# A new order of attention's steps, and the passage of an MLP to its seven products

## The chip, the cores and the metric

One core of one Trainium2 chip runs the whole program as one launch. The metric is device time in microseconds (us); lower is better. The times of the kernel before are from 3 runs: 1110.34, 1112.88 and 1113.99, so the median is 1112.88.

## What is computed

Three layers follow each other on a tensor of 4 batches, 576 positions and 512 channels (before the first layer there are 1152 positions).

```python
# 1: attention of 4 x 8 heads with 64 channels; q is averaged over pairs of positions
q_pool = q.reshape(B, H, S // 2, 2, D).mean(axis=3)          # S = 1152 -> T = 576
scores = scale * np.matmul(q_pool, k.transpose(0, 1, 3, 2))  # 576 x 1152 a head
attn   = softmax(scores);  x = attn @ v
# 2: four expert attentions (64 channels, causal), mixed by the two best gates of a position
# 3: a mixing over positions of rank 32, u = x + U, V part, and
ch  = np.maximum(u @ w_ch1, 0.0) @ w_ch2                     # 512 -> 2048 -> 512
out = u + ch
```

The two MLP matrices arrive as 64-bit floats.

## The kernel before, in words

**Precision.** Where a plain product is not accurate enough, the kernel splits an operand into a rounded high part and a low part (`cut`: ACT writes the high part, the named engine subtracts to get the low one) and multiplies three of the four combinations.

**Attention** goes over 16 pairs of heads. A pair has 2 halves of the queries (288 each) and 9 blocks of 128 keys, thus 18 units (`unit`), each with two scores (one for each head of the pair): 36 steps. `score` issues two matmuls of 128 x 288 (L606, L607) into a buffer `st` of PSUM, then ACT's exponential (L608) into `pt`, and after the second head POOL's addition to the sum `acc` (L615, L618). `pv` (L626) multiplies `pt` with the values; it is not issued unit by unit but in batches, because a group of units waits until the step that the table PV_AT gives for each unit.

Beside the 36 steps of a pair the next pair is prepared (`prep`): loads of q, k and v (`load_q`, `load_k` L482, `load_v`, one buffer for k), the sum of q's position pairs, transposes on PE (L506 for k, L515 for q), a layout of q and k by transfers from SBUF to SBUF (lines L547 to L549, L377 and L378, twelve a pair), a bound for the maximum of each row of scores (36 tests: a matmul L558 against `bd` and a DVE maximum L560) and the negated bound `nm` (L410, L412, sent on by L415). The transfers into `bd` are L537. All DMAs are issued from SP's queue in the order written, and one that waits holds up those behind it. The constants at the head of the file (LQ_AT, K_AT, SECOND_AT, ...) say at which step each piece is issued; a negative step lies in the pair before. PE, DVE and ACT take their instructions in the order written. WC_AT and WD_AT place the decoding of the first 64-bit weights (loads, and integer steps on DVE, L244 to L248) in the same steps; POST_AT places the division after a half (`post_a` L633, `post_r` L432 to L435, `post_b` L445 and L643).

**The expert attention** takes over after about 470 us with the same kind of stream; its first products read `xh` and `xl`, a cut of attention's output (`xl` on DVE at L227).

**The MLP** handles the 2304 positions in 6 groups x of 384. Groups 0 and 1 run in a base loop of T1 = 28 ticks: a tick has one up product (`up` L1199, 12 matmuls), one down product (`down` L1218, 9 matmuls, one tick after its up), and the work that the list `todo` names for the tick (`more`): decoding of a weight block, and preparations for the second part. There the groups 2 to 5 run as two passes p of 8 steps k of `seven`: seven products instead of eight on combined blocks of weights (`combine`) and of activations. The activations are transposed on PE (L1155), copied by ACT to SBUF (`lift`, L1173), and added and cut in a second step (`blend`: sums L1191 and cuts L227, shared between DVE and POOL). `seven` issues the products m5, m3, m1, m2, m4, m6, m7 (L1268) and adds them up on DVE (L1280) into four blocks that go through the ReLU and the second matrix. The products use a pool `ms` of three PSUM buffers, of which one is held as part of the output of an odd group. In this part POOL and SP also take their instructions in the order written.

Of the kernel before, what the change touches and what calls it, by code (L numbers as in the profile page):

```python
# [20 lines left out]
LQ_AT = -41  # L21
LK_AT = -19
V_AT = 5
Q_AT = [-5, -1]
K_AT = [-2, 3, 10]
LAY_AT = 18
FIRST_AT = [-33, -20, -20, -15, -10, -10, -7, -7, -6, -5, -3, 10, 13]
SECOND_AT = [-12, -9, -6, -2, 4, 11, 14, 6, 7, 9, 12, 12, 14, 15, 16, 16, 17, 17, 17, 19, 21, 21, 21, 24, 24, 25, 28, 28, 30, 31, 34, 36, 36, 36, 29, 42]
M_AT = [2, 5, 6, 7, 8, 9, 11, 12, 12, 13, 15, 16, 17, 18, 19, 20, 21, 25, 26, 28, 29, 29, 32, 32, 35, 36, 37]
F_AT = [23, 40]  # L30
PV_AT = [11, 11, 11, 16, 16, 16, 16, 31, 31, 31, 31, 31, 31, 31, 35, 35, 35, 35]
POST_AT = [[31, 32, 35], [47, 48, 53]]

WL_AT = 10
WC_AT = [10, 17, 32, 35]
WD_AT = [18, 33, 37, 39]
# [87 lines left out]
def kernel(  # L124
# [898 lines left out]
    def open_late():  # L1023
        xes.close()
        ct["cw1"] = pool(ctx, "cw1", LW)
        ct["bc"] = pool(ctx, "cbc", 8)
        ct["u"] = pool(ctx, "cu", 2)
        ct["e"] = pool(ctx, "ce", 8)
        ct["t"] = pool(ctx, "ctm", 2)
# [47 lines left out]
    def split(fi):  # L1077
        for x, g in enumerate([weights(fi, x) for x in range(2)]):
# [8 lines left out]
            "m6": (2, 0, ALU.subtract), "m7": (1, 3, ALU.subtract)}  # L1087
# [70 lines left out]
    def turn(x, c):  # L1158
# [3 lines left out]
    MOVE, STG, tn = {}, {}, [0]  # L1162
    QUAD = ((0, 0), (0, 1), (1, 0), (1, 1))
    MOVES = {"m1": (0, 3, ALU.add), "m2": (0,), "m3": (2, 3, ALU.subtract), "m4": (1, 0, ALU.subtract), "m5": (3,),
             "m6": (0, 2, ALU.add), "m7": (1, 3, ALU.add)}

    def lift(p, ci, d):

        x, h = QUAD[d]
        if d == 0:  # L1170
            STG[p, ci] = ct["bc"].tile([P, 4, TB], F32, name="sg", tag="bc") if p == 1 and ci else \
                xpool.tile([P, 4, TB], F32, name="sg", tag="x")
# [255 lines left out]
```

## Time and profile before

| what | value |
|---|---|
| median of 3 runs | 1112.88 us |
| the profiled execution | 1115.27 us |
| its span from first to last instruction | 1113.5 us |
| PE busy | 1078.2 us (97%) |
| DVE, POOL, ACT busy | 811.9, 613.1, 542.8 us |
| granted clock of PE, mean | 0.989 |

PE is the engine that is nearly always busy, so time is to be found where it waits and where the clock granted to it is below 1.00. All starts below count from the span's start. Attention's pairs follow each other about every 27.7 us, pair 0 from 18.5 us on; the MLP's base loop covers some 735 to 850 us.

### The profile page before, as it was taken

To read this page: it belongs to the slowest core of one execution; us is meant where nothing else is said; L and a number is where in the kernel's file an instruction comes from. 1 tells how busy PE (TensorE), PEld (TensorE's weight loads), DVE (VectorE), ACT (ScalarE), POOL (GpSimd) and SP (SyncE) were. 2 spreads that over 40 slices of the span, in tenths; PEclk is the share of its full clock that TensorE was granted. 3 is DMA by queue.
4 is the path that set the end of the run, shared out by engine and by line. 5 is a ranking of instruction groups with operands and counts; after the bars stand their busy time and mean duration, and the time that the engine had idled before them with its cause. 6 is when DMAs were issued, how large, how long until landed. Compare 5 with 4: busy or idle time off the path is not lost.

```text
span 1113.5 us, 19597 instructions
## 1 busy us (share of the span) xinstructions
PE 1078.2 (97%) x6652; PEld 889.9 (80%) x6652; DVE 811.9 (73%) x1707; ACT 542.8 (49%) x1361; POOL 613.1 (55%) x620
## 2 busy tenths in 40 slices
PE   6999999999999999899999998899998999999998
PEld 4777777777777777688888886699887888999987
DVE  6777777888888777566868779969879555564444
ACT  4555556555555555544555454534445445432231
POOL 5778989988887888864524244200009596800000
PEclk8999999999999999999999999999999999999999
DMA  6867888878777675012222243466665745575431
GB/s 145 193 160 179 187 197 194 182 170 187 179 172 169 159 162 129 23 35 54 63 71 59 71 134 136 139 208 199 218 203 184 241 167 196 192 265 195 165 123 58
DMA packets 135157, 171.50 MB, mean 154 GB/s; under 512 B 72464, under 2 KB 88848, under 8 KB 133008
## 3 DMA queue, kind: packets, MB, share of 16 engines
q1 hardware_dynamic: 135056, 170.24, 56.2%
q8 instruction: 53, 0.87, 0.4%
q14 instruction: 48, 0.39, 0.1%
HBM read 83.06 MB, written 32.51 MB: 104 GB/s over the span
## 4 chain that ended last, share of the span: by engine, by line
PE 82%; DVE 7%; POOL 5%; DMA 3%; issue 2%; ACT 2%; SPq 0%; POOLq 0%; ACTq 0%; DVEq 0%
PE o L1218 13%; PE pv L626 12%; PE ms L745 9%; PE ms L1268 8%; PE st L606 8%; PE ms L558 7%; PE st L607 6%; PE ms L1199 5%; PE pv L896 2%; PE ms L633 2%; PE st L871 1%; DVE mp L560 1%; POOL cb L227 1%; PE ms L506 1%; PE st L872 1%
## 5 line engine op out<-in xcount | busy, mean ns | idle before, releaser
L618 POOL TENSOR_TENSOR acc<-acc,pt 128x576 f32<-128x576 f32 x224 | 319.3, 1426 | 34.9 <-ACT pt L608 20.4
L608 ACT ACTIVATE pt<-st 128x288 f32<-128x288 f32 x576 | 219.8, 409 | 188.3 <-PE st L607 143.6
L560 DVE TENSOR_REDUCE mp<-ms 128x1 f32<-128x384 f32 x432 | 215.1, 549 | 59.8 <-PE ms L558 57.8
L626 PE MATMUL pv<-pt,vr 128*64 128x288 f32 x1152 | 154.0, 413 | 0.0
L558 PE MATMUL ms<-kn,bd 128*128 128x384 f32 x432 | 146.1, 362 | 3.9 <-DVE mp L560 1.7
L626 PEld LDWEIGHTS pv<-pt,vr 128*64 128x64 f32 x1152 | 80.7, 138 | 56.3 <-issue 5.2
L1218 PE MATMUL o<-w,hh 128*128 128x512 f32 x384 | 121.4, 396 | 1.0 <-POOL w L227 0.7
L606 PE MATMUL st<-q1a,s1a 128*128 128x288 f32 x288 | 93.7, 325 | 1.4 <-ACT pt L608 1.1
L606 PE MATMUL st<-q1b,s1b 128*128 128x288 f32 x288 | 92.7, 322 | 0.2 <-ACT pt L608 0.2
L558 PEld LDWEIGHTS ms<-kn,bd 128*128 128x128 f32 x432 | 80.7, 194 | 14.7 <-DVE mp L560 5.5
L607 PE MATMUL st<-q2a,s2a 128*128 128x288 f32 x288 | 85.4, 296 | 0.0
L607 PE MATMUL st<-q2b,s2b 128*128 128x288 f32 x288 | 85.3, 296 | 0.0
L1268 PE MATMUL ms<-bc,w 128*128 128x384 f32 x432 | 84.8, 341 | 0.0
L1218 PEld LDWEIGHTS o<-w,hh 128*128 128x128 f32 x384 | 72.1, 190 | 13.8 <-POOL w L227 1.5
L1268 PEld LDWEIGHTS ms<-bc,w 128*128 128x128 f32 x432 | 77.6, 190 | 3.0
L1218 PE MATMUL o<-w,hl 128*128 128x512 f32 x192 | 75.9, 395 | 1.2 <-DVE hl L1203 1.2
L1199 PE MATMUL ms<-uh,w 128*128 128x384 f32 x256 | 74.1, 350 | 2.8 <-POOL w L227 1.1
L606 PEld LDWEIGHTS st<-q1a,s1a 128*128 128x128 f32 x288 | 54.6, 190 | 24.2 <-issue 21.1
L888 POOL TENSOR_TENSOR acc<-acc,pt 128x576 f32<-128x576 f32 (+4 forms) x48 | 44.3, 923 | 51.0 <-ACT pt L879 49.4
L1218 PE MATMUL o<-w,hs 128*128 128x512 f32 x288 | 71.4, 393 | 0.0
L615 POOL TENSOR_TENSOR acc<-pt 128x576 f32<-128x576 f32 x32 | 50.7, 1585 | 37.3 <-ACT pt L608 37.3
L227 POOL TENSOR_TENSOR bc<-sg,bc 128x384 fp32r<-128x384 f32 x6 | 7.0, 1173 | 109.7 <-ACT bc L226 109.7
(241 smaller groups left out, 2408.3 us busy)
## 6 DMA issues: line engine op xcount, KB each, us to landing
raw<-in_moe_w_ch_dram SPq DMA_DIRECT2D x32, 512.0 KB
w_d<-cb SPq DMA_DIRECT2D x40, 256.0 KB
qr<-in_q_dram SPq DMA_DIRECT2D x16, 576.0 KB
vr<-in_v_dram SPq DMA_DIRECT2D x16, 576.0 KB
s1a<-kn SPq DMA_DIRECT2D x31, 288.0 KB
s1b<-kn SPq DMA_DIRECT2D x31, 288.0 KB
kr<-in_k_dram SPq DMA_DIRECT2D x30, 288.0 KB
wv<-v_d SPq DMA_DIRECT2D x8, 1024.0 KB
```

Source lines behind the costliest of these rows:

```text
L558: nc.tensor.matmul(ps[:, :384], BD[i % 2][:, t, :], KN[i % 2][:, c * 384:c * 384 + 384], start=True, stop=True)
L560: nc.vector.tensor_reduce(st["mp"][:, t, c:c + 1], ps[:, :384], axis=X, op=ALU.max)
L606: nc.tensor.matmul(ps[:, :HT], pr.S1[a][:, ks], pr.Q1[a][:, qs], start=True, stop=False)
L607: nc.tensor.matmul(ps[:, :HT], pr.S2[a][:, ks], pr.Q2[a][:, qs], start=False, stop=True)
L608: nc.scalar.activation(c["pt"][:, a, :], ps[:, :HT], AF.Exp, scale=0.0625)
L615: nc.gpsimd.tensor_add(t, acc[i, h], c["pt"])
L618: nc.gpsimd.tensor_add(acc[i, h], acc[i, h], c["pt"])
L626: nc.tensor.matmul(o[64 * a:64 * a + 64, :HT], vr[:, a, kt, :], c["pt"][:, a, :], start=(kt == 0), stop=(kt == NKT - 1))
L745: nc.tensor.matmul(ps, stat[x][s], mov[x][m], start=(x == 0 and y == 0), stop=(x == n - 1 and y == 2))
L1199: nc.tensor.matmul(ps[:, :TB], W[fi][:, 0, a, cs], m[:, c, :], start=(c == 0 and y == 0), stop=(c == NC - 1 and y == 2))
L1218: nc.tensor.matmul(ob[x][s_], hl[m][:, r], w2[a], start=(n == 0 and y == 0), stop=(n == NF - 1 and y == 2))
L1268: nc.tensor.matmul(ps[:, :TB], w[:, i * HD2 + c * P:i * HD2 + c * P + P], b[:, j, c, :], start=(c == 0 and y == 0), stop=(c == HC - 1 and ...
```

## The change

**Tables.** Every table of attention's order has new numbers. The batches of PV have 4, 4, 7 and 3 units (3, 4, 7 and 4 before), at steps 11, 15, 32 and 35 (11, 16, 31, 35). The layout moves from step 18 to 22, k's load from -19 to -30, and the second part of a division from 53 to 50 in the second half. Two lines of the diff stand for the rest.

```diff
-LK_AT = -19
+LK_AT = -30
-PV_AT = [11, 11, 11, 16, 16, 16, 16, 31, 31, 31, 31, 31, 31, 31, 35, 35, 35, 35]
-POST_AT = [[31, 32, 35], [47, 48, 53]]
+PV_AT = [11, 11, 11, 11, 15, 15, 15, 15, 32, 32, 32, 32, 32, 32, 32, 35, 35, 35]
+POST_AT = [[32, 33, 35], [47, 48, 50]]
...
-WC_AT = [10, 17, 32, 35]
-WD_AT = [18, 33, 37, 39]
+WC_AT = [10, 14, 30, 32]
+WD_AT = [23, 31, 34, 35]
```

**Lifts.** Two of the four blocks (d = 0 and 3) are copied to SBUF by ACT; the other two are never copied, but DVE adds them from PSUM to the copied ones. There is one lift a tick, from T1 - 9 on, and its cuts come one tick later; for the second pass there is one every second tick, with the cuts' low part on POOL. `blend` is gone.

```diff
-    def lift(p, ci, d):
+    def lift(p, ci, d, eng):
...
-        nc.scalar.activation(STG[p, ci][:, d], turn_(2 * p + x, h * HC + ci), AF.Copy)
-
-    def blend(p, ci, m, eng):
...
+        ps = turn_(2 * p + x, h * HC + ci)
+        if d in (0, 3):
+            nc.scalar.activation(sg[:, d // 3], ps, AF.Copy)
+        todo_ = {0: (), 3: (("m1", 0, ALU.add),), 1: (("m4", 0, ALU.subtract), ("m7", 1, ALU.add)),
+                 2: (("m3", 1, ALU.subtract), ("m6", 0, ALU.add))}[d]
+        ts = {}
+        for m, y, op in todo_:
+            ts[m] = ct["t"].tile([P, TB], F32, name="tb")
+            nc.vector.tensor_tensor(ts[m], ps, sg[:, y], op=op)
+
+        def rest():
+            if d in (0, 3):
+                t = move(p, ("m2", "m5")[d // 3])
+                cut(sg[:, d // 3], t[:, 0, ci], t[:, 1, ci], eng)
+            for m in ts:
+                t = move(p, m)
+                cut(ts[m], t[:, 0, ci], t[:, 1, ci], eng)
...
-    for y in range(8):
-        at(T1 - 11 + y // 2, lambda y=y: lift(1, y // 4, y % 4))
-        at(T1 + 4 + y + 10 * (y // 4), lambda y=y: lift(2, y // 4, y % 4))
-    for y in range(14):
-        m, ci = PIECES[y // 2], y % 2
-        at(T1 - 7 + y if y < 3 else T1 - 4 + (y - 3) // 3,
-           lambda y=y, m=m, ci=ci: blend(1, ci, m, nc.gpsimd if y % 3 == 1 else nc.vector))
-        at(T1 + 8 + y + 7 * (y // 7), lambda y=y, m=PIECES[y % 7]: blend(2, y // 7, m, nc.gpsimd))
+    for y, (ci, d) in enumerate((ci, d) for ci in range(HC) for d in (0, 3, 1, 2)):
+        at(T1 - 9 + y, lambda ci=ci, d=d: lift(1, ci, d, nc.vector))
+        at(T1 + 7 + 2 * y, lambda ci=ci, d=d: lift(2, ci, d, nc.gpsimd))
```

**Combined weights and temporaries.** `combine` takes its engine; for k = 0 that is DVE instead of POOL. The temporaries of `seven` get a pool of their own (`m`, 5 buffers; the pool `e` goes from 8 to 3), and some sums are made in place. The cut of the block c12 is issued before m1 instead of behind it.

```diff
-            nc.gpsimd.tensor_tensor(t, v_[:, x], v_[:, y], op=op)
+            eng.tensor_tensor(t, v_[:, x], v_[:, y], op=op)
...
-            at(s1 - 5 + y * 4 // 7, lambda k=k, m=m: combine(k, m))
+            at(s1 - 5 + y * 4 // 7, lambda k=k, m=m: combine(k, m, nc.gpsimd if k else nc.vector))
```

**Second products kept back.** The last two down products of the base loop (groups 0 and 1, block 15) are not issued at its end but handed to the first `seven`, which issues one behind m5 and one behind m1. The closing additions of groups 0 and 1 follow there.

```diff
-    def mlp(x, fi):
+    def mlp(x, fi, full=True):
         hl = up(x, fi)
-        if pend:
+        if pend and full:
             down(*pend.pop())
...
-            mlp(x, fi)
-            close()
+            mlp(x, fi, t + 1 < T1)
             more()
-        down(*pend.pop())
-        late = []
+        late = list(pend)
```

Three places of the resulting order follow. The first is SP's queue in pair 0, from the first layout of a prepared pair on (`q1a_161` to `s2b_160` are its tiles, `kr` the next keys). Before:

```order
L415 DMA q2a_149<-nm 1x4x64
L415 DMA q2b_150<-nm 1x4x64
L547 DMA q1b_162<-qh 64x576
L548 DMA q1b_162<-ql 64x576
L549 DMA q2b_164<-qh 64x576
L377 DMA s1a_157<-kn_142 64x1152 x2
L378 DMA s2a_159<-klo 64x1152
L377 DMA s1b_158<-kn_142 64x1152 x2
L378 DMA s2b_160<-klo 64x1152
L482 DMA kr<-in_k_dram 128x9x64 x2
L415 DMA q2a_163<-nm 1x5x64
L415 DMA q2b_164<-nm 1x5x64
```

And in the changed kernel, from the same load of the values on:

```order
L489 DMA vr<-in_v_dram 128x2x576
L482 DMA kr<-in_k_dram 128x9x64 x2
L415 DMA q2a_149<-nm 1x4x64
L415 DMA q2b_150<-nm 1x4x64
L547 DMA q1a_161<-qh 64x576
L548 DMA q1a_161<-ql 64x576
L549 DMA q2a_163<-qh 64x576
L547 DMA q1b_162<-qh 64x576
L548 DMA q1b_162<-ql 64x576
L549 DMA q2b_164<-qh 64x576
L377 DMA s1a_157<-kn_142 64x1152 x2
L378 DMA s2a_159<-klo 64x1152
```

The two loads of `kr` stood behind the twelve transfers of the layout and now stand ahead of them and of `nm`.

The second place is SP's queue shortly behind it, where the raw q of a later pair (`qr`) and the blocks of `bd` are moved. Before:

```order
L415 DMA q2a_163<-nm 1x5x64
L415 DMA q2b_164<-nm 1x5x64
L473 DMA qr<-in_q_dram 96x2x768
L537 DMA bd_137<-qh 64x6x64 x2
L537 DMA bd_137<-qh 64x3x64 x2
L489 DMA vr<-in_v_dram 128x2x576
```

In the changed kernel:

```order
L537 DMA bd_137<-qh 64x6x64 x2
L415 DMA q2a_163<-nm 1x5x64
L415 DMA q2b_164<-nm 1x5x64
L473 DMA qr<-in_q_dram 96x2x768
L537 DMA bd_137<-qh 64x3x64 x2
L489 DMA vr<-in_v_dram 128x2x576
```

The first transfers of `bd` were behind `qr` and are now ahead of `nm` and of `qr`.

The third place is PE where the base loop ends (`o_0_9622` to `o_2_9624` are the outputs of one group, `o_0_9942` or `o_0_9945` and so on of the other). Before, from the last down product but one on:

```order
L1218 MATMUL o_1_9623<-w,hl 128x512
L1218 MATMUL o_2_9624<-w,hh 128x512 x2
L1218 MATMUL o_2_9624<-w,hl 128x512
L1218 MATMUL o_0_9942<-w,hh 128x512 x2
L1218 MATMUL o_0_9942<-w,hl 128x512
L1218 MATMUL o_1_9943<-w,hh 128x512 x2
L1218 MATMUL o_1_9943<-w,hl 128x512
L1218 MATMUL o_2_9944<-w,hh 128x512 x2
L1218 MATMUL o_2_9944<-w,hl 128x512
L1268 MATMUL ms<-bc,cb 128x384 x6
L1268 MATMUL ms<-bc,w 128x384 x6
L1268 MATMUL ms<-bc,cb 128x384 x12
```

In the changed kernel, from the last matmul of the last up product on:

```order
L1198 MATMUL ms<-uh_9498,w 128x384
L1267 MATMUL ms<-bc,cb 128x384 x6
L1217 MATMUL o_0_9622<-w,hh 128x512 x2
L1217 MATMUL o_0_9622<-w,hl 128x512
L1217 MATMUL o_1_9623<-w,hh 128x512 x2
L1217 MATMUL o_1_9623<-w,hl 128x512
L1217 MATMUL o_2_9624<-w,hh 128x512 x2
L1217 MATMUL o_2_9624<-w,hl 128x512
L1267 MATMUL ms<-bc,w 128x384 x6
L1267 MATMUL ms<-bc,cb 128x384 x6
L1217 MATMUL o_0_9945<-w,hh 128x512 x2
L1217 MATMUL o_0_9945<-w,hl 128x512
```

The first product of `seven` (6 matmuls) now follows the last up product at once, one of the two kept-back down products stands between it and the second, and the other behind the third.

## Rows read from the trace of the kernel before

**Rows 1.** the page: busy time of each engine; one group of its fifth part
```profile
PE 1078.2 (97%) x6652; PEld 889.9 (80%) x6652; DVE 811.9 (73%) x1707; ACT 542.8 (49%) x1361; POOL 613.1 (55%) x620
...
L560 DVE TENSOR_REDUCE mp<-ms 128x1 f32<-128x384 f32 x432 | 215.1, 549 | 59.8 <-PE ms L558 57.8
```

**Rows 2.** stretches: us, busy us of each engine, PE's granted clock, DMA share, GB/s
```profile
47.60:79.00 31.40, 29.53 (x197) 22.28 (x195) 21.44 (x45) 16.01 (x45) 21.58 (x16) 0.95 0.74 163
247.44:275.16 27.72, 27.72 (x199) 21.49 (x196) 22.76 (x46) 16.25 (x47) 23.83 (x19) 1.00 0.80 187
330.50:359.70 29.20, 28.26 (x200) 21.60 (x196) 25.77 (x49) 15.82 (x45) 23.41 (x18) 1.00 0.72 168
```

**Rows 3.** timeline of PE, pair 0: start, us, engine, line, tiles [idle before]
```profile
53.94 0.52 PE L506 MATMUL ms<-ident,kr 128*128 128x128 f32 x3 [1.78 <-DVE xt L643]
...
54.82 3.85 PE L626 MATMUL pv<-pt,vr 128*64 128x288 f32 x16
...
69.44 2.16 PE L626 MATMUL pv<-pt,vr 128*64 128x288 f32 x16
```

**Rows 4.** timeline of SP's transfer issues, pair 0
```profile
44.91 2.91 SPq L482 DMA_DIRECT2D kr<-in_k_dram  x2
```

**Rows 5.** waits of PE in pair 3: engine, line, releaser, us, times, longest
```profile
PE ms L558 <- DMA bd<-qh: 1.2, 1, 1.2
```

**Rows 6.** timeline of DVE and PE, pair 10 and an earlier pair
```profile
235.73 0.17 DVE L434 TENSOR_SCALAR d<-d 128x9 f32<-128x9 f32 x1
...
346.70 1.45 DVE L434 TENSOR_SCALAR d<-d 128x9 f32<-128x9 f32 x1
...
348.86 0.45 PE L558 MATMUL ms<-kn,bd 128*128 128x384 f32 x1 [0.74 <-DVE mp L560]
```

**Rows 7.** timeline of DVE and PE, passage to the second attention
```profile
458.06 7.19 DVE L227 TENSOR_TENSOR xl<-xt,xh 128x576 fp32r<-128x576 f32 x4 [2.24 <-ACT xh L226]
465.18 0.47 DVE L445 STREAM_TRANSPOSE d<-d 128x288 f32<-128x288 f32 x1
465.68 0.75 DVE L643 TENSOR_TENSOR xt<-pv,d 128x288 f32<-128x288 f32 x1
...
463.43 0.41 PE L745 MATMUL ms<-xl,wqk 128*128 128x320 f32 x1 [0.66 <-DVE xl L227]
...
465.31 0.42 PE L745 MATMUL ms<-xl,wqk 128*128 128x320 f32 x1 [1.18 <-DVE xl L227]
```

**Rows 8.** timeline of PE and DVE, passage to the seven products
```profile
848.26 0.50 PE L1218 MATMUL o<-w,hl 128*128 128x512 f32 x1 [0.93 <-DVE hl L1203]
...
856.54 1.84 PE L1268 MATMUL ms<-bc,cb 128*128 128x384 f32 x6 [3.24 <-DVE c L1280]
...
855.93 0.56 DVE L1280 TENSOR_TENSOR c<-ms,m5s 128x384 f32<-128x384 f32 x1 [0.75 <-ACT m3s L1277]
```

**Rows 9.** chain that ended last, same passage: start, us, what
```profile
853.63 1.14 POOL tw L1123
...
856.54 3.76 PE ms L1268 x12
```

**Rows 10.** the same chain in ticks of the base loop
```profile
785.63 2.08 PE o L1218 x9
787.71 2.12 PE ms L1199 x12
...
805.62 0.34 PE ms L1155 x3
```

**Rows 11.** a tick without lifts, and one with two
```profile
783.52:787.71 4.19, 4.19 (x23) 3.80 (x22) 3.78 (x8) 1.89 (x5) 0.00 (x0) 1.00 0.91 254
...
803.52:808.89 5.37, 5.12 (x29) 4.43 (x28) 3.70 (x7) 2.45 (x5) 0.00 (x0) 1.00 0.15 59
```

**Rows 12.** DVE by line and form, 829 to 856: busy us, mean ns
```profile
L1191 DVE TENSOR_TENSOR tb<-sg 128x384 f32<-128x384 f32 x4 | 4.5, 1160 | 0.0
```

**Rows 13.** timeline of DVE, tick 26
```profile
835.39 0.55 DVE L227 TENSOR_TENSOR bc<-u,bc 128x384 fp32r<-128x384 f32 x1
```

More of the change, by code (lines that the diff above doesn't have):

```diff
@@ L1027, in open_late @@
         ct["u"] = pool(ctx, "cu", 2)
[L1028 to L1029 removed]
+        ct["e"] = pool(ctx, "ce", 3)
+        ct["m"] = pool(ctx, "cm", 5)
+        ct["t"] = pool(ctx, "csg", 2)
     W, V1 = {}, {}
@@ L1160, in turn, with move @@
         cut(turn_(x, c), UH[x][:, c, :], UL[x][:, c, :])
-    MOVE, STG, tn = {}, {}, [0]
+    MOVE, STG = {}, {}
     QUAD = ((0, 0), (0, 1), (1, 0), (1, 1))
-    MOVES = {"m1": (0, 3, ALU.add), "m2": (0,), "m3": (2, 3, ALU.subtract), "m4": (1, 0, ALU.subtract), "m5": (3,),
-             "m6": (0, 2, ALU.add), "m7": (1, 3, ALU.add)}
-    def lift(p, ci, d):
[L1169 to L1172, printed above, removed]
-        nc.scalar.activation(STG[p, ci][:, d], turn_(2 * p + x, h * HC + ci), AF.Copy)
-    def blend(p, ci, m, eng):
-        if ci == 0:
+    def move(p, m):
+        if (p, m) not in MOVE:
             n = PIECES.index(m)
@@ L1180, in blend @@
             MOVE[p, m] = q.tile([P, 2, HC, TB], F32R, name="bc", **kw)
-        d, sg = MOVE[p, m], STG[p, ci]
-        if len(MOVES[m]) == 1:
-            t = sg[:, MOVES[m][0]]
-        else:
-            tn[0] += 1
-            if p == 1 and tn[0] % 2:
-                t = SPARE[0][:, tn[0] // 2 % 2]
-            else:
-                t = ct["t"].tile([P, TB], F32, name="tb")
-            x, y, op = MOVES[m]
-            eng.tensor_tensor(t, sg[:, x], sg[:, y], op=op)
-        return lambda: cut(t, d[:, 0, ci], d[:, 1, ci], eng)
+        return MOVE[p, m]
+    def lift(p, ci, d, eng):
+        x, h = QUAD[d]
+        if d == 0:
+            STG[p, ci] = ct["t"].tile([P, 2, TB], F32, name="sg", bufs=1)
+        sg = STG[p, ci]
+        ps = turn_(2 * p + x, h * HC + ci)
[14 more added lines that the diff above has]
+                cut(ts[m], t[:, 0, ci], t[:, 1, ci], eng)
+        return rest
     def up(x, fi):
@@ L1287, in seven @@
         mul("m3")
-        copy("m3")
-        add("c12", "m3", "m5s")
+        copy("m3", "c22")
+        add("c12", "m3", "c11")
+        h12 = spread_h(s["c12"])
         mul("m1")
-        add("c22", "m1", "m3s")
-        add("c11", "m1", "m5s", ALU.subtract)
-        h12 = spread_h(s["c12"])
+        add("c11", "m1", "c11", ALU.subtract)
+        add("c22", "m1", "c22")
         if late:
@@ L1298, in seven @@
         mul("m2")
-        copy("m2")
-        add("c22", "c22", "m2", ALU.subtract)
+        copy("m2", "c21")
+        nc.vector.tensor_tensor(s["c22"], s["c22"], s["m2"][:, :TB], op=ALU.subtract)
         mul("m4")
-        add("c21", "m4", "m2s")
-        add("c11", "c11", "m4")
+        add("c21", "m4", "c21")
+        add("c11", "m4", "c11")
         h21 = spread_h(s["c21"])
```

78 lines of the change are left out of this document (35 added, 43 removed).

## The prediction

> **What bounds the kernel now.** I read the page first: PE is busy 1078.2 of 1113.5 us [rows 1], so all its idle time is 35.3 us. DVE is next with 811.9. A change that leaves PE's matmuls as they are (this one does: the same products in another order) can win only from that idle time and from stretches in which PE ran at its lower clock; it can lose only where PE comes to wait. So I went through PE's waits and matmul times stage by stage. The reader is to see three things. A steady pair of heads lasts 27.72 us with PE busy all of it [rows 2]. Pairs 0 and 10 of the same work last longer, and each contains a wait of PE [rows 2]. And the longest wait outside the start, 3.24 us, stands where the MLP goes over to the seven products [rows 8].
>
> **Steady pairs.** PV batches of 3, 4, 7, 4 units become 4, 4, 7, 3: four batches before and after, so PE changes from scores to PV as often. With PE busy all 27.72 us there is no idle time to remove; price 0. It would cost something only if a moved step made PE wait (rival 1).
>
> **Pair 0.** PE stops 1.78 us before the transposes of kr [rows 3]. The row names DVE's xt, but that product was long done; by the order these transposes wait for the two loads of kr. SP issued those only at 44.91 [rows 4], because they stand behind the twelve transfers that lay out q and k, and behind two of nm between them. After the stop the 16-matmul PV batch took 3.85 us [rows 3]; a batch of the same form took 2.16 at 69.44 [rows 3], and the granted clock, 1.00 (2.4 GHz) all through a steady pair, is 0.95 as a mean of this stretch, so that part of it ran at 1.2 GHz [rows 2]. So the stop costs 1.78 + 1.69 = 3.5 us, and the 31.40 us of this stretch less 27.72 (3.7) agrees. In the changed order the loads of kr stand ahead of nm and of the twelve transfers: −3.5. What becomes late next are those transfers, now behind nm and behind kr's 2.91 us of issuing; see rival 3.
>
> **Pair 3.** PE waits 1.2 us for bd [rows 5]. In the new queue the first loads of bd stand ahead of qr: −1.2.
>
> **Pair 10.** It takes 29.20 against 27.72 [rows 2], 1.5 us more. Half is one wait for DVE's maxima, 0.74 [rows 6]; there DVE spent 1.45 us on a scaling of 9 columns, which took 0.17 at 235.73 [rows 6]. The decoding steps (WC) move away from this place, ahead of the batches, but still in every pair; I take 60%: −0.9, with ends 0 and −1.5.
>
> **To the second attention.** DVE's four subtractions xl take 7.19 us in a row, and PE waits 0.66 and 1.18 us on the last two [rows 7]. The second part of the division (transpose 0.47 and product 0.75, [rows 7]) moves from behind the fourth xl to between the second and the third. PE then gets the third and fourth 1.22 us later: +1.2.
>
> **Start.** The first steps move from ahead of the first pair into it (11 negative places, now 7). Four tests of 549 ns [rows 1] are 2.2 us that DVE no longer has to do before the first scores, and has to do during them; nothing in the trace of before shows which wins. Price 0, ends −2.2 and +2.2.
>
> Attention: −3.5 − 1.2 − 0.9 + 1.2 = −4.4.
>
> **The turn to the seven products.** PE waits 0.93 for hl and 3.24 for c [rows 8], and the 12 matmuls after the second wait take 3.76 us [rows 9] against 2.12 for 12 matmuls of the same 384 columns earlier [rows 10], 1.6 us more. Sum 0.93 + 3.24 + 1.6 = 5.8; I count 5.6. The chain behind it: c at 855.93 waited 0.75 us for ACT's copy [rows 8], which stood behind ACT's half of a cut that waited for POOL's tw, 1.14 us from 853.63 [rows 9]; and DVE's own additions were slow, 1160 ns each in this stretch [rows 12] against 0.56 us for 128x384 at 855.93 [rows 8]. Three parts of the change meet here. Two second products of 9 matmuls, 2.08 us each [rows 10], now stand inside the first seven, one behind m5 and one behind m1: 4.2 us of matmuls whose operands are ready, more than the longest wait. The combination for k = 0 goes from POOL to DVE, ticks earlier. And POOL has nothing left to do there, so DVE's additions get their short time. −5.6. The work itself is not less; only the wait is filled.
>
> **Lifts.** A tick without a lift takes 4.19 us, PE busy all of it; one with two takes 5.37 [rows 11]: 1.18 more, of which two times 0.34 are the transposes [rows 10] and the other 0.5 is PE waiting for ACT's copy of the second one, and slower matmuls behind it. Four ticks with two lifts become eight with one, which I count as the transposes alone: 4 × (1.18 − 0.68) = −2.0.
>
> **What DVE gets for it.** In these ticks DVE decodes weights: 3.78 us busy of 4.19 [rows 11]. Now come ten sums and fourteen subtractions at about 0.55 us (what 128x384 took at 855.93, where one operand lies in PSUM, [rows 8]) and twelve operations for k = 0, over eight ticks; before, a third of the blends ran on POOL and the rest in later ticks. With 2, 4, 4 and 3 additional operations, ticks 20 to 23 want about 4.9, 6.0, 6.0 and 5.4 us of DVE, PE some 4.5 each (4.19 and a lift's transposes): DVE falls behind by 0.4 + 1.5 + 1.5 + 0.9 = 4.3 us. PE waits for DVE only by w and hl, which are a tick ahead, so part of it is absorbed, and in ticks 24 to 27 less is decoded. Ends 0 and +4.3; I take the middle and a little more, +2.4, since both w and hl stand in DVE's queue behind the sums.
>
> On this the Trainium skill speaks against the change: "VectorE: DVE Perf Modes", section "Rules for kernel authors", would have a matmul's result copied to SBUF first where many operations follow, and "Perfetto Trace Analysis", section "Optimizing Scalar/DVE Operations", states a fixed cost of about 60 ns on SBUF and 125 on PSUM. By that the ten sums would take an estimated 0.65 us more. The trace shows no such difference here: 0.56 us with an operand in PSUM (c at 855.93), 0.55 with both in SBUF (bc at 835.39) [rows 8, 13]; without it the sum stays.
>
> **The sum.** Tail: −5.6 − 2.0 + 2.4 = −5.2. Both: −9.6. Every pair's order is new, and the trace of before cannot show the new order's small waits; I add two of the size of 0.74: +1.5. That leaves −8.1: the profiled execution of 1115.27 us (span 1113.5 and 1.8 around it) would take 1107.2. It was 2.4 above the median of the runs, 1112.88, so the median becomes 1104.8.
>
> **Rivals.** *1. The new order makes PE wait in every pair.* The second batch comes at step 15 and the third at 32, so 17 steps without a batch instead of 15, in which DVE has twelve tests and the sum of q to do, before ten and the second scaling. If PE comes to wait for a maximum once a pair, at the price of 1.18 (what DVE's lateness cost at 465.31, [rows 7]), 14 pairs are 16.5 us: 1121.3. It is slower than before from (1116.2 − 1104.8) / 14 = 0.8 us a pair. For it: DVE is busy 22.76 of 27.72 us already [rows 2], and one slow operation was enough in pair 10. Against: in the steady pair DVE has 5 us to spare, and the second scaling has moved ahead of the batch. *2. DVE becomes the bound in ticks 20 to 27.* If the sums take 1160 ns as beside POOL [rows 12], ten sums are 6 us more, none absorbed: 1104.8 + 6 = 1110.8. For it: 3.78 of 4.19 is nearly full. Against: POOL is idle in the decoding ticks (0.00, [rows 11]). The Trainium skill has a reason for such long times: "Perfetto Trace Analysis", section "Optimizing Scalar/DVE Operations", says that GpSimd and DVE share a read port of SBUF, so that work moved between them might not help. The trace agrees, with 1160 ns beside 560; and by it the emptier POOL speaks for the forecast. *3. The kr loads come no sooner, or the layout comes too late.* If kr is limited by the transfers on the DMA engines (0.74 busy in that stretch, [rows 2]) and not by its place in the queue, −3.5 is lost: 1108.3; if also the pair after it waits for its layout, by as much as PE waited for kr, 1.8 more, 1110.1.
>
> **How the numbers follow.** About 0.3% (3.3 us) is what a measurement here can tell, so faster is below 1109.5 and slower above 1116.2. Forecast 0.70, rival 1 0.09, rival 2 0.10, rival 3 0.11. Own range of the forecast: the terms with open ends (pair 10 +0.9/−0.6, start ±2.2, DVE +1.9/−2.4, small waits ±1.5) add to +6.5 and −6.7 if all go one way: 1098.1 to 1111.3. Range 1098 to 1111, which takes in rivals 2 and 3 and leaves out most of rival 1. Faster: forecast 0.66, rival 3 0.08, rival 2 0.04: 0.78. Same: 0.04 + 0.06 + 0.03 + 0.02 from rival 1: 0.15. Slower: 0.07.
>
> **What would show it.** In the profile after: no wait before the first kr transposes of pair 0 and a PV batch near 2.1 us there; no wait on bd in pair 3; longer waits at xl; a steady pair still at 27.7; the waits of 3.24 and 0.93 gone and the 12 matmuls behind m1 near 2.1; ticks with a lift near 4.5, with some PE waits on DVE in ticks 20 to 23. I would be wrong in kind if the steady pair got longer than 28, and in the tail if PE waited on w or hl for more than 4 us in sum.

## The result, and the profile after

The changed kernel takes 1102.89 us (median of 6 runs, 1100.99 to 1104.41), the kernel before 1112.27 in the same session (6 runs, 1110.34 to 1113.99). The ratio is 0.9916, 95% interval 0.9901 to 0.9932: 9.4 us faster. The forecast was 1104.8, 8.1 us less than before.

The profiled executions differ by more: from first to last instruction 1113.5 us before and 1099.2 after, and 1110.9 in a second profile of the kernel before, taken later. The columns below differ by 14.3 and 11.7 us in sum, not by 9.4, because the profile after is of the fastest of its six runs and the first one before is of an execution slower than all six (1115.27). The table cuts the three traces at the same instructions (first score of a pair, first up product of a tick, first product of a `seven`); the base loop's tick 0 starts at 723.0, not near 735 as I wrote above.

| stretch, us | before | before, second profile | after |
|---|---|---|---|
| to the first score | 18.50 | 18.16 | 18.14 |
| pair 0 | 40.10 | 38.02 | 37.34 |
| pairs 1 to 5 | 141.22 | 140.84 | 138.31 |
| pairs 6 to 10 | 138.39 | 138.43 | 138.16 |
| pair 11 | 29.18 | 29.19 | 27.64 |
| pairs 12 to 14 | 81.97 | 82.02 | 81.94 |
| pair 15 to attention's last score | 31.77 | 31.83 | 32.97 |
| to the base loop | 241.88 | 241.95 | 240.32 |
| base loop, tick 0 | 5.85 | 5.86 | 4.28 |
| ticks 1 to 26 | 113.66 | 113.64 | 113.09 |
| tick 27 and the first `seven` | 24.04 | 24.04 | 18.62 |
| the rest | 246.93 | 246.90 | 248.41 |

(What the forecast called pairs 3 and 10 are pairs 4 and 11 here, counted from 0.) The page of the kernel after, first part, beside [rows 1]: PE has 8 us less of busy time for the same 6652 matmuls. In these two profiles part of the difference is thus clock and not waiting. The first one before has four stretches of 3.4 us at a granted clock of 0.50 (1.2 GHz) from pair 0 to the first `seven`: from 55.0, 686.4, 724.0 and 857.1 us on; the second has the last three of them, the one after none. At half the clock each costs an estimated 1.7 us.

```profile
PE 1070.2 (97%) x6652; PEld 882.6 (80%) x6652; DVE 811.5 (74%) x1737; ACT 542.4 (49%) x1353; POOL 578.5 (53%) x590
```

Pair 0 in the timeline of PE after, beside [rows 3]: the kr transposes follow without a wait, and the PV batch behind them has 12 matmuls and the short time.

```profile
53.45 0.49 PE L506 MATMUL ms<-ident,kr 128*128 128x128 f32 x3
53.87 1.68 PE L626 MATMUL pv<-pt,vr 128*64 128x288 f32 x12
```

Two pairs after, by stretch (columns as in [rows 2]). PE is busy all of both; the second is the one that took 29.20 before.

```profile
276.68:304.33 27.65, 27.65 (x199) 21.47 (x197) 24.72 (x49) 16.04 (x45) 23.25 (x17) 1.00 0.72 172
331.95:359.59 27.64, 27.64 (x198) 21.46 (x196) 21.48 (x45) 16.68 (x46) 24.67 (x18) 1.00 0.72 173
```

The passage to the second attention in the timeline of DVE and PE, beside [rows 7]: transpose and product now stand between the xl, and PE waits 1.18 us twice.

```profile
450.99 4.00 DVE L227 TENSOR_TENSOR xl<-xt,xh 128x576 fp32r<-128x576 f32 x2 [2.24 <-ACT xh L226]
454.91 0.47 DVE L445 STREAM_TRANSPOSE d<-d 128x288 f32<-128x288 f32 x1
455.41 0.68 DVE L643 TENSOR_TENSOR xt<-pv,d 128x288 f32<-128x288 f32 x1
455.93 2.84 DVE L227 TENSOR_TENSOR xl<-xt,xh 128x576 fp32r<-128x576 f32 x2
...
456.94 0.41 PE L745 MATMUL ms<-xl,wqk 128*128 128x320 f32 x1 [1.18 <-DVE xl L227]
...
458.82 0.42 PE L745 MATMUL ms<-xl,wqk 128*128 128x320 f32 x1 [1.18 <-DVE xl L227]
```

Ticks 21 to 24, by stretch, beside [rows 11]. PE is idle for part of the last two (4.84 busy of 5.52, 4.77 of 4.92), and DVE is busy for 5.42 of 5.52: the backlog that was forecast, though for ticks 20 to 23.

```profile
803.51:808.01 4.50, 4.50 (x27) 4.08 (x26) 4.40 (x10) 2.59 (x6) 0.00 (x0) 1.00 0.94 357
808.01:812.71 4.70, 4.70 (x28) 3.98 (x26) 4.60 (x11) 2.22 (x6) 0.00 (x0) 1.00 0.62 196
812.71:818.23 5.52, 4.84 (x26) 4.04 (x25) 5.42 (x12) 2.52 (x7) 0.00 (x0) 1.00 0.97 308
818.23:823.15 4.92, 4.77 (x26) 4.08 (x24) 4.82 (x11) 2.30 (x6) 0.00 (x0) 1.00 0.09 35
```

PE's waits there and in the first `seven` (timeline), beside [rows 8]. In tick 23 PE waits 0.68 us for a buffer of `ms` that DVE's sums still read. In the first `seven` the waits of 3.24 and 0.93 us are gone, and 0.48 is left, for DVE's closing additions.

```profile
817.86 0.52 PE L1149 MATMUL ms<-ident,u 128*128 128x128 f32 x3 [0.68 <-DVE tb L1181]
...
844.47 0.70 PE L1217 MATMUL o<-w,hh 128*128 128x512 f32 x2 [0.48 <-DVE u L1227]
```

And the chain that ended last through the first `seven`, beside [rows 9]: the kept-back product stands between m5 and m3, and two products (12 matmuls) take 2.12, not 3.76.

```profile
834.55 1.04 PE ms L1267 x6
835.59 2.08 PE o L1217 x9
837.68 1.07 PE ms L1267 x6
...
846.80 2.12 PE ms L1267 x12
```

### The profile page after: what moved, and what is told of

It is laid out like the page before. It is cut to its first block, busy times and chain, and to the rows that moved or that the text cites. A ratio compares the mean times of both kernels' runs of the same rounds, so it can differ in the third digit from the quotient of the medians.

```text
span 1099.2 us, 19629 instructions
## 1 busy us (share of the span) xinstructions
PE 1070.2 (97%) x6652; PEld 882.6 (80%) x6652; DVE 811.5 (74%) x1737; ACT 542.4 (49%) x1353; POOL 578.5 (53%) x590
## 4 chain that ended last, share of the span: by engine, by line
PE 88%; DVE 8%; ACT 1%; issue 1%; POOL 1%; DMA 0%; ACTq 0%; DVEq 0%; POOLq 0%
PE o L1217 15%; PE pv L626 13%; PE ms L1267 10%; PE ms L745 10%; PE st L606 8%; PE ms L558 7%; PE st L607 7%; PE ms L1198 5%; PE pv L896 2%; PE ms L633 2%; PE st L871 1%; PE ms L506 1%; PE st L872 1%; PE ms L817 1%; PE pv L948 1%; DVE u L1227 1%
## 5 line engine op out<-in xcount | busy, mean ns | idle before, releaser
L618 POOL TENSOR_TENSOR acc<-acc,pt 128x576 f32<-128x576 f32 x224 | 319.0, 1424 | 35.7 <-ACT pt L608 20.0
L558 PE MATMUL ms<-kn,bd 128*128 128x384 f32 x432 | 151.8, 364 | 1.9 <-DVE mp L560 1.3
L1124 POOL TENSOR_TENSOR tw<-wv 128x256 f32<-128x256 f32 x35 | 30.0, 864 | 117.1 <-DVE cb L227 117.1
L606 PE MATMUL st<-q1b,s1b 128*128 128x288 f32 x288 | 90.2, 313 | 0.1
L1278 DVE TENSOR_TENSOR c<-ms,c 128x384 f32<-128x384 f32 x96 | 50.3, 551 | 48.0 <-ACT c L1275 47.6
```

What stands on the lines that cost most here:

```text
L558: nc.tensor.matmul(ps[:, :384], BD[i % 2][:, t, :], KN[i % 2][:, c * 384:c * 384 + 384], start=True, stop=True)
L606: nc.tensor.matmul(ps[:, :HT], pr.S1[a][:, ks], pr.Q1[a][:, qs], start=True, stop=False)
L618: nc.gpsimd.tensor_add(acc[i, h], acc[i, h], c["pt"])
L1278: nc.vector.tensor_tensor(s[dst] if dst in s else tmp(dst), s[m][:, :TB], s[y], op=op)
```

## The experiments

Each was timed against the kernel before on the same chip; a ratio below 1 is faster, and its 95% interval stands in brackets. The median of the kernel before was 1111.27 us beside the two halves, the late kr and the division at step 53; 1112.24 beside the division moved in one pair and the three edits of the MLP; and 1112.98 beside the early kr, the earlier cut, the old batches and the unchanged kernel. The unchanged kernel, run again under another name, came out at 0.9986 (0.9972 to 0.9999), which says what a ratio here can mean.

**The two halves apart.** The new tables in the kernel before:

```diff
-LK_AT = -19
-PV_AT = [11, 11, 11, 16, 16, 16, 16, 31, ...]
+LK_AT = -30
+PV_AT = [11, 11, 11, 11, 15, 15, 15, 15, 32, ...]
...
```

> The kernel before with the new tables of attention's order alone; the MLP as before. Theory (the terms add up, each in its stage): attention gains in pairs 0 to 4 and 11 and loses 1.2 us at the passage to the second attention, 4.4 to 6.6 us in sum: 1106 to 1108 us; the end of the attention's last score 4.4 to 6.6 us earlier than in the kernel before, the wait of 3.2 us at the passage to the seven products still there. Rival (the two parts depend on each other: the tail's gain comes from what attention leaves over, or the 3.1 us that the two profiles differ by in the 40 us before the base loop belong to the tables): 1103 to 1105 us.

Measured 1107.86 (before 1111.27), ratio 0.9967 (0.9952 to 0.9981). Attention's last score comes 4.7 us earlier than in the first profile of before, 2.1 than in the second; the tail is as before, with the 3.2 us wait. The theory's range holds; of the rival one sign is there as well: the 3.1 us by which the profiles in the table differ ahead of tick 1 are gone in this one. And the old tables in the changed kernel:

```diff
-LK_AT = -30
-PV_AT = [11, 11, 11, 11, 15, 15, 15, 15, 32, ...]
+LK_AT = -19
+PV_AT = [11, 11, 11, 16, 16, 16, 16, 31, ...]
...
```

> The changed kernel with the old tables of attention's order: the MLP's changes alone. Theory: the tail gains 4.8 to 5.2 us and nothing else changes: 1107 to 1108 us; PE's 1.8 us wait before the transposes of kr in pair 0 is there again. The 3.1 us by which the two profiles differ between the last expert's attention and the base loop are scatter of a run and come and go without either part. Rival: they belong to the MLP's change (its pools are laid out in another way), then 1103 to 1105 us, and that stretch is as short here as in the changed kernel.

Measured 1107.41, ratio 0.9973 (0.996 to 0.9986). From tick 1 to the end it gains 4.5 us (384.63 to 380.17), just as the changed kernel does (380.12); PE waits 1.53 us for kr in pair 0. So each half is worth some 3 to 4 us alone, and the intervals leave it open whether the 2 us between their sum and 9.4 are more than scatter. The 3.1 us ahead of tick 1 are gone in both profiles, so neither half alone is needed for that.

**Where kr stands in the queue.** The changed kernel with kr's load late:

```diff
-LK_AT = -30
+LK_AT = -19
```

> The changed kernel with the load of kr at its old place (step -19 and not -30), nothing else. Theory (place in the queue decides): in pair 0 the loads stand behind the layout's twelve transfers again, PE waits 1.5 to 2 us for them and runs at the lower clock behind that: 2.8 to 3.5 us slower than the changed kernel, 1105.5 to 1106.5. Rival (the transfer engines' load decides, or the later layout made the gain): within 1 us of the changed kernel, 1102 to 1104.

Measured 1102.97, ratio 0.9929 (0.9914 to 0.9944): my theory fell. Timeline of SP and PE of this run:

```profile
44.04 2.95 SPq L482 DMA_DIRECT2D kr<-in_k_dram  x2
...
53.89 0.49 PE L506 MATMUL ms<-ident,kr 128*128 128x128 f32 x3
```

kr is issued as late as before (44.04 against 44.91), and PE doesn't wait, because in the new order it comes to the transposes at 53.89 and not at 52.16 (53.94 less the wait). The kernel before with kr early, and nothing else:

```diff
-LK_AT = -19
+LK_AT = -30
```

> The kernel before with the load of kr at step -30 and not -19, nothing else. Theory (here kr's place in the queue behind the layout is what PE waits for): no wait ahead of the kr transposes of pair 0, 1.3 to 1.8 us less than the kernel before: 1109 to 1111. Rival (the layout, now behind kr, becomes late, or kr lands late anyway): no gain, 1111 to 1113, with a wait of PE in pair 0 or 1 on kr or on the layout.

Measured 1112.80 (before 1112.98), ratio 1.0002 (0.9991 to 1.0012). Timeline of PE:

```profile
52.54 0.49 PE L506 MATMUL ms<-ident,kr 128*128 128x128 f32 x3
...
113.99 0.41 PE L558 MATMUL ms<-kn,bd 128*128 128x384 f32 x1 [1.40 <-DMA bd<-qh]
```

The place in the queue does take the wait from pair 0 (37.06 us, 0.96 less than in the second profile of before), but PE then waits 1.40 us for bd in pair 3, where that profile has a wait of 0.32 at the same test, and pair 3 is 1.1 us longer. In this profile the gain is given back later, by the same queue. The forecast's term holds as a mechanism; alone it is worth no more than the interval leaves open, about 1 us.

**The division's second part.** Back to step 53, in every pair:

```diff
-POST_AT = [[32, 33, 35], [47, 48, 50]]
+POST_AT = [[32, 33, 35], [47, 48, 53]]
```

> The changed kernel with the second part of the division in the second half at step 53 again and not 50. Theory: at the passage to the second attention the four subtractions xl stand together again, PE gets them 1.2 us earlier: 1101.7, nothing lost in the pairs. Rival (the earlier place is what spares the wait in pair 11 or frees PV's PSUM buffer in time): a steady pair gets longer, and the time is 1103 or more.

Measured 1116.06, ratio 1.0045 (1.0028 to 1.0062): 13 us slower than the changed kernel, and slower than before. A steady pair takes 28.54 us. Timeline of DVE and PE in one:

```profile
297.45 0.56 DVE L560 TENSOR_REDUCE mp<-ms 128x1 f32<-128x384 f32 x1 [1.72 <-PE ms L558]
297.92 0.47 DVE L445 STREAM_TRANSPOSE d<-d 128x288 f32<-128x288 f32 x1
298.43 0.70 DVE L643 TENSOR_TENSOR xt<-pv,d 128x288 f32<-128x288 f32 x1
298.98 1.46 DVE L560 TENSOR_REDUCE mp<-ms 128x1 f32<-128x384 f32 x3
...
299.56 0.45 PE L558 MATMUL ms<-kn,bd 128*128 128x384 f32 x1 [0.56 <-DVE mp L560]
```

PE stands in the batch of step 15 (DVE idle for 1.72 us), then issues tests; DVE has one of them, the two operations of the division (1.17 us), and only then the next three. PE waits 0.56 us for a free buffer; from start to start the tests around this wait lie 1.16 us apart, their neighbours 0.45. It is the forecast's first rival, at 0.89 us a pair (28.54 less 27.65), and one number in a table keeps it away. And in the last but one pair alone, behind the xl:

```diff
-                (ends if g is post[0] else later).setdefault(w + t, []).append(g)
+                (ends if g is post[0] else later).setdefault(w + t + (4 if t == 50 and u // per == n // per - 2 else 0), []).append(g)
```

> The changed kernel with the second part of the division of the last but one pair alone four steps later, behind the four subtractions xl. Theory (the two operations between the xl cost PE 1.2 us, and after two waits of 1.18 us PE runs at the lower clock in most runs, 1.4 us more): PE waits about 1.2 us there and not 2.4, 1100.5 to 1102. Rival (PE is held by the slow xl beside POOL's additions, whatever stands between): 1102.5 to 1103.5. The price that every pair paid in the run with step 53 is not expected, since the last pair prepares no other.

Measured 1101.51 (4 runs), ratio 0.991 (0.9894 to 0.9926). By the median alone the theory could stand; the timeline of DVE and PE says otherwise:

```profile
450.83 7.77 DVE L227 TENSOR_TENSOR xl<-xt,xh 128x576 fp32r<-128x576 f32 x4 [2.25 <-ACT xh L226]
...
456.77 0.42 PE L745 MATMUL ms<-xl,wqk 128*128 128x320 f32 x1 [1.17 <-DVE xl L227]
...
458.65 0.41 PE L745 MATMUL ms<-xl,wqk 128*128 128x320 f32 x1 [1.17 <-DVE xl L227]
```

The same two waits stand at the same distance. The four xl, now together, take 7.77 us; with the division between they took 6.84, but 7.78 from the first's start to the last's end. So the division's two operations cost the xl nothing. In both profiles POOL makes four additions meanwhile, 7.08 us in sum; that these set the pace is likely by the rows, and was not tested by itself. On top of that, the cut four steps earlier:

```diff
-XC_AT = [12, 13, 14, 15]
+XC_AT = [8, 9, 10, 11]
...
-    place(side, [(11, open_right)], n * (NP - 1))
+    place(side, [(7, open_right)], n * (NP - 1))
```

> The run with the late last division, and in addition the cut of attention's output for the second attention (xh, xl) four steps earlier in the last pair, steps 8 to 11. Theory (PE waits for xl because DVE starts on them late, behind ACT's xh, and takes 1.8 to 2 us each beside POOL's additions): xl start some 2 us earlier, PE's two waits of 1.18 us go, and with them the lower clock behind them: 1099 to 1101. Rival (earlier, ACT's xh hold back the exponentials and PE waits for those instead): 1102 to 1104, with waits of PE's scores on ACT.

Measured 1103.03, ratio 0.9906 (0.9889 to 0.9922). The rival's time came, but not by its cause; timeline of DVE, ACT and PE:

```profile
447.07 5.57 DVE L227 TENSOR_TENSOR xl<-xt,xh 128x576 fp32r<-128x576 f32 x4 [2.32 <-ACT xh L226]
...
454.26 0.44 ACT L439 ACTIVATE d<-d 128x288 f32<-128x288 f32 x1 [3.67 <-DVE d L435]
...
455.06 1.82 PE L626 MATMUL pv<-pt,vr 128*64 128x288 f32 x6 [2.28 <-ACT pt L608]
```

The waits for xl are gone, the xl are shorter (5.57), and PE waits 2.28 us in one piece for an exponential, in a PV batch and not at a score. That exponential does not stand behind ACT's xh, which are long done, but behind ACT's operation of the division (L439), which waits 3.67 us for DVE's reciprocal (L435), and that stands behind the four xl. So 2.36 us of waiting became 2.28.

**The batches.** The old ones under the new tables:

```diff
-PV_AT = [11, 11, 11, 11, 15, 15, 15, 15, 32, 32, 32, 32, 32, 32, 32, 35, 35, 35]
+PV_AT = [11, 11, 11, 16, 16, 16, 16, 31, 31, 31, 31, 31, 31, 31, 35, 35, 35, 35]
```

> The changed kernel with the old batches of PV (3, 4, 7 and 4 units at steps 11, 16, 31 and 35), all other tables new. Theory (the batches as such are worth nothing, PE is busy all through a steady pair): pairs of 27.6 to 27.7 us, 1102 to 1104. Rival (the other tables are fitted to batches at 15 and 32; the old ones put a test or a transpose behind a batch and PE waits for DVE in every pair): 28.0 us a pair or more, 1107 and up.

Measured 1109.59, ratio 0.9979 (0.9969 to 0.9988): the rival's numbers, but not its cause. Pairs got longer by 0.3 to 0.7 us, but PE waits for nothing, as the stretch of one pair shows:

```profile
308.36:336.31 27.95, 27.95 (x199) 21.35 (x197) 25.06 (x49) 16.16 (x45) 23.28 (x17) 1.00 0.71 169
```

The timeline of PE shows what it does with the time: the sums of the division (L633, at step 32) have lost their batch and stand apart.

```profile
327.91 3.62 PE L626 MATMUL pv<-pt,vr 128*64 128x288 f32 x28
...
331.91 0.71 PE L633 MATMUL ms<-acc,ones 128*64 128x288 f32 x4
```

In the changed kernel they run straight into the batch:

```profile
324.64 0.71 PE L633 MATMUL ms<-acc,ones 128*64 128x288 f32 x4
325.18 3.56 PE L626 MATMUL pv<-pt,vr 128*64 128x288 f32 x28
```

By these rows the lengthening, about 0.37 us a pair and 5.5 us over 15 pairs, is one more change of PE to products of the form 128*64 and back; nothing else in the pair's rows got longer. So the old batches as such were not tested free of that; the kernel before had its sums and its batch both at step 31.

**The passage to the seven products.** Without the products kept back:

```diff
-            mlp(x, fi, t + 1 < T1)
+            mlp(x, fi)
...
-        late = list(pend)
+        down(*pend.pop())
+        late = []
```

> The changed kernel with the last two second products issued at the end of the base loop again, not inside the first seven. Theory (both parts of the change count: the products kept back cover a wait that the combination on DVE has made shorter): PE waits 1 to 3 us behind m1 or m3 of the first seven, 1104 to 1106.5. Rival A (the products kept back made all of the 5.4 us there): 1107 to 1108.5, with a wait near 3.2 us and matmuls at the lower clock behind it. Rival B (moving the combination to DVE made it all): 1102.5 to 1103.5.

Measured 1105.24, ratio 0.9938 (0.9925 to 0.9952). Timeline of PE:

```profile
847.57 1.32 PE L1267 MATMUL ms<-bc,w 128*128 128x384 f32 x6 [0.88 <-DVE c L1278]
850.05 0.70 PE L1217 MATMUL o<-w,hh 128*128 128x512 f32 x2 [1.16 <-DVE u L1227]
```

From tick 27 to the end of the first `seven` 2.1 us are lost, these two waits and no lower clock behind them. With the products kept back but the combination on POOL again:

```diff
-combine(k, m, nc.gpsimd if k else nc.vector)
+combine(k, m, nc.gpsimd)
```

> The changed kernel with the combination for k = 0 on POOL again. Theory (the two kept-back products cover the chain over POOL; DVE gets slow operations beside POOL, but twelve fewer of them): 1102 to 1105, DVE's additions and cuts of 128x384 beside POOL at 0.9 to 1.2 us and not 0.55. Rival (POOL's combination is the late part and 4.2 us of products do not cover it): a wait of 1 us or more of PE on c in the first seven, 1105 to 1108.

Measured 1103.73, ratio 0.9925 (0.9911 to 0.9939). Timeline of PE:

```profile
848.17 0.70 PE L1217 MATMUL o<-w,hh 128*128 128x512 f32 x2 [0.96 <-DVE u L1227]
```

Here 0.5 us are lost (0.96 for 0.48 before the same product) and next to nothing in the ticks. So of the 5.4 us at this place either edit brings most without the other, with the rest of the change in place: 3.3 without the kept-back products, 4.9 without the combination on DVE. They are not additive. No run left out both, so what the rest of the change does there alone stays open.

**The order of the lifts.**

```diff
-    for y, (ci, d) in enumerate((ci, d) for ci in range(HC) for d in (0, 3, 1, 2)):
+    for y, (ci, d) in enumerate(((0, 0), (0, 3), (1, 0), (1, 3), (0, 1), (0, 2), (1, 1), (1, 2))):
         at(T1 - 9 + y, lambda ci=ci, d=d: lift(1, ci, d, nc.vector))
...
```

> The changed kernel with the lifts of the first pass in another order: the four that only copy or add once first, the four with two sums last, when fewer weights are decoded (the copied blocks of this pass in buffers of the pool m). Theory (DVE's backlog in ticks 20 to 24 is what PE waits for, 3.4 us less the transposes of lifts): ticks 20 to 24 last 4.5 to 4.7 us each, 1 to 2 us of the backlog goes: 1101 to 1102. Rival (the backlog only moves to the ticks with the combination, or the ticks are long for another reason): 1102.5 to 1104.

Measured 1103.15, ratio 0.9919 (0.9901 to 0.9937). Ticks 22 to 24 by stretch:

```profile
808.43:812.93 4.50, 4.50 (x27) 4.06 (x26) 4.17 (x9) 2.47 (x6) 0.00 (x0) 1.00 0.60 188
812.93:817.43 4.50, 4.50 (x27) 4.08 (x26) 4.40 (x10) 2.55 (x6) 0.00 (x0) 1.00 1.02 310
817.43:822.97 5.54, 4.94 (x27) 3.99 (x25) 5.44 (x13) 3.00 (x8) 0.00 (x0) 1.00 0.37 148
```

Ticks 22 and 23 fall to 4.50 as the theory wants, and tick 24 takes 5.54. Net 0.6 us less in this profile, too little for the median, which lies in the rival's range: half theory, half rival.

**The second profile of before.**

> The kernel before, unchanged, for a second profile. Theory: four places in which the first profile of this kernel was longer than every later one (pair 11 by 1.2 to 1.5 us, and three stretches ahead of the base loop by 0.7, 0.8 and 1.6) are scatter of that execution, and so is the batch of 3.85 us behind the wait for kr; here they are short, and this profile lies 3 to 5 us under the first one. Rival: they belong to this kernel and show again.

Measured 1111.94. Timeline of PE and DVE:

```profile
53.20 0.52 PE L506 MATMUL ms<-ident,kr 128*128 128x128 f32 x3 [0.96 <-DMA kr<-in_k_dram]
...
54.09 2.16 PE L626 MATMUL pv<-pt,vr 128*64 128x288 f32 x16
...
343.95 1.44 DVE L434 TENSOR_SCALAR d<-d 128x9 f32<-128x9 f32 x1
```

In pair 0 the theory holds: PE waits 0.96 us for kr, the batch takes 2.16, and the pair is 2.1 us shorter than in the first profile. In pair 11 and ahead of tick 1 it fell: both are as long as in the first one, and the scaling of 9 columns takes 1.44 us again.

No version measured here beats the changed kernel beyond its interval.

## Why the prediction was right, and where its steps were not

The time came out 1.9 us under the forecast (the gain is 1.3 us larger), and the two large causes were named: the turn to the seven products, and waits in attention. That the sum came so near has luck in it. Against the first profile, from which the terms were priced, the stages differ by 14.3 us and not by 8.1; terms that were too small or left out (pairs 1 to 5, pair 11, the 3.1 us ahead of tick 1) stand against terms that were too dear (pair 0, the small waits, DVE's backlog), and the rest is how far each profile lies from the median of its kernel.

**Pair 0: right sign, wrong size.** −3.5 was forecast; −2.8 against the first profile, −0.7 against the second. The step that failed is "So the stop costs 1.78 + 1.69": the second figure, the lower clock behind the stop, came up in one of three profiles with that wait (0.96 and 1.53 us in the others, batches of 2.16). Even the −0.7 is within what profiles differ by: pair 0 takes 37.34 to 38.43 us in the ten profiles with the new tables. And "behind the twelve transfers" was one way only: the transposes' own later place removes the wait without it.

**Start and steady pairs: right.** 0 was forecast for both. Up to the first score −0.4 (first profile) and 0.0 (second) were measured, over the five pairs 6 to 10 together −0.2 and −0.3.

**Pairs 1 to 5: too small.** −1.2 for bd; measured −2.5 to −2.9, of which the stretch with the bd wait has 0.9 to 1.4, and four small excesses that I left out the rest.

**Pair 11: too small, and for another reason.** −0.9 was forecast out of 1.5, for the decoding steps that move away; all 1.5 went. But a profile of the old tables with the new MLP has 27.98 for this pair, and of before with kr early 27.72, so the DVE operation of 1.45 us that makes it does not stand in every run of the old tables. What makes it long is POOL: beside the scaling of [rows 6], from 346.70 to 348.15, the timeline of POOL before has an addition from 346.69 to 348.11.

```profile
346.69 1.42 POOL L618 TENSOR_TENSOR acc<-acc,pt 128x576 f32<-128x576 f32 x1
```

In the trace of before, all 30 of the 48 scalings that take over 0.3 us end 0.03 us behind the end of an operation on POOL, and none of the 18 short ones lies inside one. So the excess of pair 11 hangs on where POOL's addition happens to begin: the scaling takes 1.45 and 1.44 us in the two profiles with 29.2 us, and 0.17 in the two of the old tables without the excess.

**To the second attention: right size in this profile, wrong reason.** +1.2 was forecast and +1.1 to +1.2 measured, but "PE then gets the third and fourth 1.22 us later" is refuted by the run that moved the division away. What lengthens the stretch at the full clock are its PV matmuls. From start to start they take 1.3 us more of it, while PE's idle time there is nearly the same (3.26 us, 3.02 before). There are 60 of them and not 56, since one more unit stands ahead of the last batch. And the second batch, now at step 15, takes 3.1 us up to the next score, where it took 2.1 at step 16: its last matmuls wait for ACT's exponentials, which alternate with the xh at that place. Timeline of PE before, then after:

```profile
458.84 2.16 PE L626 MATMUL pv<-pt,vr 128*64 128x288 f32 x16
```

```profile
450.57 2.31 PE L626 MATMUL pv<-pt,vr 128*64 128x288 f32 x14
453.05 0.70 PE L626 MATMUL pv<-pt,vr 128*64 128x288 f32 x2 [0.17 <-ACT pt L608]
```

In six of the ten profiles with the new tables this stretch takes 34.3 to 35.7 us, 1.3 to 2.7 more than here. What the rows show there is the clock: between 455 and 463 us the changed kernel's profile has it at 1.00 (2.4 GHz), the one with kr late, with the same two waits just before, at 0.79, so partly at 1.2 GHz (below, after and kr late). All six have a stretch at 0.50 there, and the three profiles with the same two waits and 33.0 us have none.

```profile
455.00:463.00 8.00, 5.64 (x40) 5.12 (x39) 4.65 (x6) 2.10 (x7) 3.85 (x3) 1.00 0.14 33
714.82:719.10 4.28, 4.28 (x22) 3.91 (x23) 2.38 (x5) 1.05 (x2) 0.90 (x1) 1.00 0.62 234
```

```profile
455.00:463.00 8.00, 5.64 (x30) 5.12 (x30) 4.47 (x6) 1.70 (x5) 3.31 (x2) 0.79 0.10 22
```

**The turn to the seven products: right.** −5.6 forecast, −5.4 measured. Two of the three parts that I let "meet" do the same work twice. Here the lower clock behind the wait was no accident of one execution: it came in all four profiles that have this wait of 3.2 to 3.3 us (before twice, kr early, the tables alone).

**Lifts right, DVE's backlog too dear.** −2.0 + 2.4 forecast, −0.6 measured: ticks 17 to 20 gain 4.0 and ticks 21 to 26 lose 3.4 (transposes moved there included). By the forecast's own count, 4.19 a tick and 0.34 a lift's transposes, the lifts gain 1.9 and the backlog costs 1.4. One step of it was wrong: "PE waits for DVE only by w and hl". The longest wait, 0.68 us in tick 23, is for a PSUM buffer, since DVE now reads the transposes straight from PSUM and releases them late. Sums with an operand in PSUM took 0.55 us, as the forecast said; the 65 ns more that the figures of the Trainium skill ("Perfetto Trace Analysis", section "Optimizing Scalar/DVE Operations") would give each of them do not show. (The rule that the forecast set against the change, in "VectorE: DVE Perf Modes", section "Rules for kernel authors", names the operand in PSUM as its other choice, so nothing here refutes it.)

**Small waits: +1.5 forecast, and +1.5 measured at another place, by chance.** The term stood for new waits in attention's pairs, and there it was wrong: the pairs got shorter, and no wait of PE over 0.2 us is left in pairs 1 to 14. The 1.5 us were lost behind the first `seven`, around the second pass's lifts: in three of these eight places the next product starts 0.63 to 0.84 us after the transposes do, where before it was 0.24 to 0.41 in all eight. That it was this place was not foreseen.

**What the sum left out** are 3.1 us ahead of tick 1. Half of them is tick 0, a stretch at a granted clock of 0.71 in the second profile of before (below), against 1.00 after (second row of the stretches after, above):

```profile
720.44:726.30 5.86, 5.86 (x22) 5.40 (x22) 2.66 (x6) 1.04 (x2) 0.91 (x1) 0.71 0.55 206
```

It is long in the two profiles of before, in the one with kr early and in the one with the old batches under the new tables, short in the ten others, old tables or new. The waits of PE just ahead of it do not decide it: 0.52, 0.56 and 0.57 us stand there in all fourteen. What does was not found. The other half lies ahead of tick 0. About 0.8 us of it goes with another stretch at 0.50 (from 686.4 us in the first profile), and 0.8 with a step of decoding that took DVE 1.38 us in both profiles of before and with kr early, and 0.43 in the other eleven profiles; it, too, ended only when POOL's operation had. Timeline of POOL and DVE before:

```profile
712.01 1.35 POOL L227 TENSOR_TENSOR w<-dcb,w 128x512 fp32r<-128x512 f32 x1 [3.57 <-ACT w L226]
...
712.26 1.38 DVE L245 TENSOR_SCALAR dca<-dca 128x512 int32<-128x512 int32 x1
```

Rival 1 did not come, but would have without one edit of the change, and its break-even of 0.8 us a pair was met by the run at step 53 (0.89, slower than before). Rival 2 fell: DVE's sums took 0.55 us, though DVE held PE in ticks 23 and 24. Rival 3 did not come; something like its second half came in the old order alone, where PE waited for bd once kr's loads stood early.

## What to carry to other kernels

Take a second profile before pricing a wait: the wait for kr (0.96 to 1.78 us) returned each time, the lower clock behind it in one profile of three, while behind the wait of 3.2 to 3.3 us it came in four of four. A table of steps is priced as a whole: one entry moved back cost 13 us, more than the whole change brings, and one group parted from its neighbour 0.37 us a pair, over half of it in sum, with PE busy all the while. Where two edits fill the same hole, take one away at a time before adding their gains.

## What was not expected of the hardware

A scaling of 9 columns on DVE (L434, from SBUF to SBUF) takes 0.17 us, or lasts until POOL's running operation ends: in all fourteen traces each one that takes over 0.3 us (1.45 us in pair 11 of before) ends 0.02 to 0.04 us behind the end of an operation of POOL. DVE's maxima, which read PSUM, don't show this: all 432 of before take at most 0.57 us, though 226 of them lie inside an operation of POOL.

Operations of DVE with two SBUF operands took longer beside POOL's additions: four xl took 7.77 us in a row, and 5.57 when they came four steps earlier, where POOL's additions have pauses. The Trainium skill ("Perfetto Trace Analysis", section "Optimizing Scalar/DVE Operations") names a read port shared by GpSimd and DVE, and these numbers agree.
